# Attention and mixture of experts on one core: expert slots in another order, results fetched ahead of the next tokens

## The chip, the core and the metric

The kernel runs on one core of a Trainium2 chip. The metric is the device time of one execution in microseconds; lower is better. The core has TensorE (PE in the rows; its weight loads are PEld), VectorE (DVE), ScalarE (ACT), GpSimd (POOL) and SyncE (SP), each with its own instruction stream in order; they meet at semaphores. Transfers are issued by SP (and, for scattered rows, by GpSimd) and carried by 16 shared DMA engines.

## The reference

First an attention without softmax over 8 batches of 2496 tokens, then a layer of 8 experts, of which each token visits one.

```python
scores = scale * np.matmul(z, z.transpose(0, 2, 1))      # scale = 1 / S, S = 2496, z: (8, 2496, 64)
attn = np.maximum(scores, 0.0) ** 2
x = (u * np.matmul(attn, v)).reshape(B * S, D)            # 19968 tokens, D = 256
...
logits = x @ w_gate
e_idx = np.argmax(logits, axis=1)                         # the token's expert, of E = 8
...
for e in range(E):
    mask = e_idx == e
    h = np.maximum(x[mask] @ w1[e], 0.0)                  # 256 -> 1024
    out[mask] = gate_w[mask, None] * eom[mask, e, None] * (h @ w2[e])   # 1024 -> 256
```

## The kernel before

**Attention** takes the first 1320 us or so. Its finished tokens are sorted: GpSimd scatters each row of x, with its gate factor and its number, into `xs` in DRAM, where each expert has a region of its own.

**Slots.** The experts then run as slots. A slot is a piece of one expert's region, of a width n fixed when the kernel is built; which expert and which rows is read on the chip from small tables. There are 27 wide slots of 512 tokens from table 0 (made from the counts of the first seven batches), 3 more wide ones (table 1), seven of 480, 448, 416, 384, 352, 320 and 288 tokens (table 2), and 8 of 256 (table 3), in that order; ten further slots of 256 lie behind a condition. The last piece of an expert's tokens is covered by one of the seven, so that little is padded.

**One slot** (class `Slot`, the slot's number is `g`): `load_x` reads two values from the table and starts four transfers `sx<-xs` and one or two for `meta` (factor and number of each token). `load_w` starts eight transfers `raw<-in_w` of 256 KB, a first half `W1` and a second `W2`. There are two sets of raw buffers, so a slot's weights overwrite those of the slot two before it; if that had the same expert, a flag in the table (`cond`) skips the transfers. `split_w` cuts each weight tile into a rounded part (a ScalarE cast, L830) and the rest (a VectorE subtraction, L831). `turn` and `split_x` do the like for the tokens. `up` runs 48 matmuls in eight PSUM banks of a pool of three (`sc`, L872; two groups to a bank at 256 tokens); each bank gives `hh` (ScalarE, L881) and `hl` (VectorE, L882). `down` runs 48 more matmuls (`o`), in two halves.

**Results.** A slot of 256 has its result with tokens on partitions and scales it at once. The wider ones come out turned: VectorE transposes each half to `yt` (L945, L947), SP stores it to `yd` in DRAM (L951 to L954), and during the next slot SP reads it back in another shape, `ym` (`collect`, L967); ScalarE multiplies it by the factors (`scale`, L977, `y<-ym`) and GpSimd scatters the rows to the output.

**Order of the work.** All five engines run in the order written. `run` goes over the slots; during slot i it prepares i+1 (`split_w`, `turn`, `split_x`) and loads i+2. `up` and `down` call `then()` after each bank and twice after each half: steps 0 to 7 and 8 to 11 of a slot (six steps at 256 tokens). Each `then()` first takes one entry of the list `later`, which holds the end of attention, the making of tables 1 to 3 (`other_tables`, some twenty pieces of small VectorE instructions) and the zero rows behind each expert's last token (`pads`, nine transfers of 528 KB), and then what was put at this step with `at`. Loads of slot i+2 stand in front of step 0, its `W2` at step 3.

Of the kernel before, what the change touches and what calls it, by code (L numbers as in the profile page):

```python
# [10 lines left out]
I32 = mybir.dt.int32  # L11
AF = mybir.ActivationFunctionType
ALU = mybir.AluOpType
# [25 lines left out]
N_MAIN = 8  # L39
N_REST = MOST // E - 2 * N_FULL  # L40
LENGTHS = (N_FIRST, N_FULL, N_MID, N_REST)
WIDTHS = [TW] * (N_FIRST + N_FULL) + MID[::-1] + [T] * N_REST
NSLOT = sum(LENGTHS)
N_EXTRA = N_REST - N_MAIN

HALF = 1

# [12 lines left out]
def attention_moe(ctx, tc, zt, zq_in, ut, v, wg, w12, out):  # L60
# [437 lines left out]
    def t1(name, shape, dt=F32, tag=None):  # L498
        return pool.tile([1] + shape, dt, name=name, tag=tag or name)
# [23 lines left out]
    for i, n in enumerate(LENGTHS):  # L523
        body = n - (N_EXTRA if i == 3 else 0)
        half = -(-body // 2)
        si = t1(f"sl_i{i}", [max(n, 2 * half)], I32)
        nc.gpsimd.iota(si[:, 0 : 2 * half], pattern=[[1, half], [half, 2]], base=0, channel_multiplier=0)
        if n > 2 * half:
            nc.gpsimd.iota(si[:, 2 * half : n], pattern=[[1, n - 2 * half]], base=2 * half, channel_multiplier=0)
        elif n > body:  # L530
            nc.gpsimd.iota(si[:, body:n], pattern=[[1, n - body]], base=body, channel_multiplier=0)
        if i == 2:
            nc.gpsimd.iota(si[:, 0:n], pattern=[[-1, n]], base=n - 1, channel_multiplier=0)
        sl = t1(f"sl{i}", [n])
        nc.vector.tensor_copy(out=sl, in_=si[:, 0:n])
        places.append(sl)
# [2 lines left out]
    e8 = t1("e8", [E])  # L539
    nc.vector.tensor_copy(out=e8, in_=e8_i)  # L540

    def table(i, size, upto, step, base0, before):

        n, sl = LENGTHS[i], places[i]
        yield
        past = t1("past", [n, E])  # L550
        nc.vector.tensor_tensor(
            out=past,
            in0=sl.unsqueeze(2).to_broadcast([1, n, E]),
            in1=upto.unsqueeze(1).to_broadcast([1, n, E]),
            op=ALU.is_ge,
        )
        yield
        ex_f = t1("ex_f", [n + 2])
        if before is not None:
            nc.vector.tensor_copy(out=ex_f[:, 0:2], in_=before)  # L560
        ex_v = ex_f[:, 2:]
        nc.vector.tensor_reduce(out=ex_v.unsqueeze(2), in_=past, op=ALU.add, axis=AX.X)
        nc.vector.tensor_scalar(out=ex_v, in0=ex_v, scalar1=float(E - 1), scalar2=None, op0=ALU.min)
        yield
        nc.vector.tensor_tensor(
            out=past, in0=past, in1=step.unsqueeze(1).to_broadcast([1, n, E]), op=ALU.mult
        )
        yield
        off = t1("off", [n, 1])
        nc.vector.tensor_reduce(out=off, in_=past, op=ALU.add, axis=AX.X)  # L570
        nc.vector.tensor_scalar(out=off, in0=off, scalar1=base0, scalar2=None, op0=ALU.add)
        row = t1("row_f", [n])
        nc.vector.scalar_tensor_tensor(
            out=row, in0=sl, scalar=float(size), in1=off.rearrange("p a b -> p (a b)"), op0=ALU.mult, op1=ALU.add
        )
        yield
        return write(i, row, ex_f, before)

    def write(i, row, ex_f, before):
        name, n, ex_v = f"tab{i}", LENGTHS[i], ex_f[:, 2:]  # L580
        tab = t1(name, [3, n], I32)
        nc.vector.tensor_scalar(out=tab[:, 0], in0=row, scalar1=float(E * CAP), scalar2=None, op0=ALU.min)
        nc.vector.tensor_copy(out=tab[:, 1], in_=ex_v)
        if before is None:
            nc.vector.memset(tab[:, 2, 0:2], 1)
            nc.vector.tensor_tensor(out=tab[:, 2, 2:], in0=ex_v[:, 2:], in1=ex_v[:, : n - 2], op=ALU.not_equal)
        else:
            nc.vector.tensor_tensor(out=tab[:, 2], in0=ex_v, in1=ex_f[:, 0:n], op=ALU.not_equal)
        last = t1(name + "_last", [2])
        nc.vector.tensor_copy(out=last, in_=ex_f[:, n : n + 2])  # L590
        return tab, last

    def steps(name, row, n, size):

# [31 lines left out]
    def first_table():  # L626
        cnt = t1("cnt0", [E])
        nc.vector.tensor_tensor(out=cnt, in0=carry[0][0:1], in1=base9[:, 0:E], op=ALU.subtract)
        ns = rounded("ns0", cnt, TW, 0)
        upto = running("upto0", ns)  # L630
        st = steps("st0", base9, ns, TW)
        tabs[0], tabs["last"] = yield from table(0, TW, upto, st, 0.0, None)
        tabs["rest"] = behind("rest0", base9, capped("taken0", ns, upto, N_FIRST), TW)

    def other_tables():
# [79 lines left out]
        yield  # L715
        st = steps("st1", base1, full, TW)
        upto = running("upto1", full)
        tabs[1], tabs["last"] = yield from table(1, TW, upto, st, base1[:, 0:1], tabs["last"])
        yield
        n, sl = LENGTHS[2], places[2]  # L720
        which = t1("which", [n, E])
# [3 lines left out]
            in1=kind_of.unsqueeze(1).to_broadcast([1, n, E]),  # L725
            op=ALU.is_equal,
        )
        ex_f = t1("ex_f", [n + 2])
        nc.vector.tensor_copy(out=ex_f[:, 0:2], in_=tabs["last"])
        part = t1("part", [n, E])  # L730
        nc.vector.tensor_tensor(out=part, in0=which, in1=e8.unsqueeze(1).to_broadcast([1, n, E]), op=ALU.mult)
        nc.vector.tensor_reduce(out=ex_f[:, 2:].unsqueeze(2), in_=part, op=ALU.add, axis=AX.X)
        yield
        nc.vector.tensor_tensor(
            out=part, in0=which, in1=rest[:, 0:E].unsqueeze(1).to_broadcast([1, n, E]), op=ALU.mult
        )
        row = t1("row_f", [n])
        nc.vector.tensor_reduce(out=row.unsqueeze(2), in_=part, op=ALU.add, axis=AX.X)
        tabs[2], tabs["last"] = write(2, row, ex_f, tabs["last"])
        yield  # L740
        base3 = behind("base3", base1, full, TW)
        ns = t1("ns3", [E])
# [2 lines left out]
        upto = running("upto3", ns)  # L745
        used = tabs["used"] = t1("used", [1], I32)
        nc.vector.tensor_copy(out=used, in_=upto[:, E - 1 : E])
        tabs[3], _ = yield from table(3, T, upto, st, base3[:, 0:1], tabs["last"])

    def pads():  # L750

# [20 lines left out]
    class Slot:  # L772
        def __init__(self, g):
            self.g = g
            self.part = next(p for p in range(len(LENGTHS)) if g < sum(LENGTHS[: p + 1]))
            self.i = g - sum(LENGTHS[: self.part])
            self.n = WIDTHS[g]
            self.w = [None] * 8

        def value(self, k, top):  # L780
# [32 lines left out]
        def load_w(self, js):  # L813
            if not hasattr(self, "ex"):
                self.ex = self.value(1, E - 1)
                self.kw = {"cond": self.value(2, 1)} if 2 <= self.g <= NSLOT - N_EXTRA else {}
            wr = raw[self.g % 2]
            for j in js:
                if self.g < 2:
                    wr[j] = pool.tile([P, CH], F32, name=f"raw{j}", tag="two", bufs=16)  # L820
                nc.sync.dma_start(  # L821
                    out=wr[j],
                    in_=w12[bass.ds(self.ex, 1), :, j * CH : (j + 1) * CH].rearrange("e p f -> (e p) f"),
                    **self.kw,
                )
# [269 lines left out]
    parts = []  # L1095
    later = [idle, tail.advance] * (TAIL - 1) + [idle, lambda: parts.extend(tail.scatter())]
    later += [idle, lambda: parts.pop(0)()] * 4
    later += [idle] * (5 * 12 - len(later))
    more, fill = other_tables(), pads()
    for _ in range(27):  # L1100
        later += [idle, lambda: next(more, None), idle]
    for _ in range(E + 2):
        later += [lambda: next(fill, None)] + [idle] * 11

    def run(part, ahead=None):

        late = [j for j in W2 if part[0].w[j] is None]
        every = part + ([ahead] if ahead else [])
        for i, s in enumerate(part):
            nx = every[i + 1] if i + 1 < len(every) else None  # L1110
            nn = every[i + 2] if i + 2 < len(every) else None

            long = s.n > T
            steps = [[] for _ in range(12 if long else 6)]

            def at(k, *what):
                steps[k] += what

            for j in late:
                at(j % 4, lambda j=j: s.split_w([j]))  # L1120
            late = []
            if i and part[i - 1].n > T:
                at(2 if long else 1, part[i - 1].collect)
                at(9 if long else 4, part[i - 1].scale)
            if nn:
                nn.load_x()
                nn.load_w(W1)
                at(3, lambda: nn.load_w(W2))
            if nx:
                w = [lambda j=j: nx.split_w([j]) for j in range(8)]  # L1130
                for k, what in enumerate(
                    ([w[0]], [w[1]], [w[2]], [w[3]], [nx.turn], [w[4]], [], [], [nx.split_x], [w[5]], [w[6]], [w[7]])
                    if long
                    else ([w[0]], [w[1]], [nx.turn], [w[2]], [nx.split_x, w[3], w[4]], w[5:])
                ):
                    at(k, *what)

            def then():
                if later:
                    later.pop(0)()  # L1140
                for what in steps.pop(0):
                    what()

            s.up(then)
            s.down(then)
# [70 lines left out]
```

## Time and profile before

| what | us |
|---|---|
| median of 3 runs | 2237.5 (2236.78 to 2239.54) |
| the profiled execution, its own time | 2220.67 |
| its span | 2219.0 |
| TensorE busy | 2186.8 (99%) |
| VectorE busy | 1760.8 (79%) |
| ScalarE busy | 1441.4 (65%) |
| GpSimd busy | 935.8 (42%) |

Busy time is summed over the whole span, so 99% says nothing of single stretches. The granted clock of TensorE is 0.994 in the mean; 1 stands for 2.4 GHz, 0.5 for 1.2 GHz. The profiled execution is 16.8 us shorter than the median of the runs.

### The profile page before, as it was taken

The numbers are of one execution on the slowest core, as the hardware profiler recorded it, in microseconds if no ns is written. First come the engines' busy times: TensorE is split into PE (matmuls) and PEld (weight loads), VectorE is DVE, ScalarE is ACT, GpSimd is POOL, SyncE is SP. The second block draws the span as 40 slices with busy tenths as digits, with TensorE's granted clock in tenths as the row PEclk, the third lists the DMA queues.
The fourth block names the chain that finished last, engine by engine and source line by source line (L and its number), as shares of the span: only waits on it lengthen the run. The fifth ranks groups of instructions, "written<-read, shape, count | busy, mean of one in ns | idle before, by whom it ended". The sixth has DMA issues, their size and how long they took to land. (4 is left out here: it accounts for less than half of the span.)

```text
span 2219.0 us, 34158 instructions
## 1 busy us (share of the span) xinstructions
PE 2186.8 (99%) x10290; PEld 1851.4 (83%) x10290; DVE 1760.8 (79%) x2929; ACT 1441.4 (65%) x2271; POOL 935.8 (42%) x809
## 2 busy tenths in 40 slices
PE   9999999999999999999999999999999999999888
PEld 7888888888888888888888878888888888889888
DVE  8889889889889889889889886667566666666566
ACT  8767767767767767767767754545455555555555
POOL 0265565465566466466566565221212121111221
PEclk9999999999999999999999999999999999999999
DMA  6794794784785775876866884535554545666552
GB/s 203 190 224 157 195 218 165 202 204 167 212 190 182 208 179 193 214 163 205 211 167 202 224 162 118 154 86 143 143 144 142 146 114 166 185 193 188 160 155 63
DMA packets 435138, 384.94 MB, mean 173 GB/s; under 512 B 140637, under 2 KB 353502, under 8 KB 434944
## 3 DMA queue, kind: packets, MB, share of 16 engines
q1 hardware_dynamic: 407360, 341.09, 57.5%
q0 software_dynamic: 27584, 41.58, 6.2%
q8 instruction: 83, 1.36, 0.3%
q14 instruction: 111, 0.91, 0.1%
HBM read 281.98 MB, written 148.90 MB: 194 GB/s over the span
## 5 line engine op out<-in xcount | busy, mean ns | idle before, releaser
L467 POOL DMA_INDIRECT xs<-xr,idx x624 | 764.8, 1226 | 612.9 <-DVE idx L460 414.0
L289 PE MATMUL o<-ah,v 128*128 128x512 f32 (+1 forms) x3200 | 968.7, 386 | 0.8 <-DVE v L187 0.8
L289 PEld LDWEIGHTS o<-ah,v 128*128 128x128 f32 x3200 | 598.7, 188 | 110.0 <-DVE v L187 2.2
L289 PE MATMUL o<-al,v 128*128 128x512 f32 (+1 forms) x1520 | 586.5, 386 | 0.6 <-DVE al L226 0.3
L987 POOL DMA_INDIRECT out<-y,meta x160 | 168.1, 1051 | 660.4 <-ACT y L977 564.6
L881 ACT ACTIVATE hh<-sc 128x512 fp32r<-128x512 f32 (+7 forms) x328 | 190.4, 581 | 295.7 <-PE sc L872 294.7
L872 PE MATMUL sc<-xh,w 128*128 128x512 f32 (+8 forms) x1440 | 360.1, 366 | 17.4 <-DVE hl L882 12.0
L217 ACT ACTIVATE a<-sc 128x512 f32<-128x512 f32 (+1 forms) x480 | 251.3, 576 | 174.2 <-PE sc L216 173.2
L934 PE MATMUL o<-hh,w 128*128 128x512 f32 (+7 forms) x1184 | 357.9, 379 | 0.0
L226 DVE TENSOR_TENSOR al<-a,ah 128x1024 fp32r<-128x1024 f32 (+1 forms) x232 | 274.2, 1182 | 87.0 <-ACT ah L222 80.5
L289 PEld LDWEIGHTS o<-al,v 128*128 128x128 f32 x1520 | 285.7, 188 | 56.5 <-DVE al L226 3.2
L872 PEld LDWEIGHTS sc<-xh,w 128*128 128x128 f32 x1440 | 258.1, 191 | 60.0 <-DVE hl L882 14.8
L831 DVE TENSOR_TENSOR w<-raw,w 128x512 fp32r<-128x512 f32 x368 | 244.7, 678 | 54.4 <-ACT w L830 54.3
L934 PEld LDWEIGHTS o<-hh,w 128*128 128x128 f32 x1184 | 220.1, 188 | 38.8
L220 ACT ACTIVATE a<-a 128x1024 f32<-128x1024 f32 (+1 forms) x240 | 246.2, 1026 | 7.6
L882 DVE SCALAR_TENSOR_TENSOR hl<-sc,hh 128x512 fp32r<-128x512 f32 (+7 forms) x328 | 216.1, 661 | 43.7 <-ACT hh L881 34.8
L934 PE MATMUL o<-hl,w 128*128 128x512 f32 (+7 forms) x592 | 224.4, 379 | 0.0
L830 ACT CAST w<-raw 128x512 fp32r<-128x512 f32 x368 | 216.2, 613 | 0.0
L872 PE MATMUL sc<-xl,w 128*128 128x512 f32 (+8 forms) x720 | 204.3, 365 | 0.0
L945 DVE STREAM_TRANSPOSE yt<-o 128x512 f32<-128x512 f32 (+2 forms) x74 | 50.4, 681 | 176.4 <-PE o L934 160.5
L215 PE MATMUL sc<-z,hl 128*128 128x512 f32 (+1 forms) x480 | 184.0, 383 | 2.6 <-ACT a L217 1.8
L216 PE MATMUL sc<-z,hl 128*128 128x512 f32 (+1 forms) x480 | 183.1, 381 | 0.0
(185 smaller groups left out, 2419.0 us busy)
## 6 DMA issues: line engine op xcount, KB each, us to landing
raw<-in_w SPq DMA_DIRECT2D x368, 256.0 KB
td<-t SPq DMA_DIRECT2D x160, 512.0 KB
z<-td SPq DMA_DIRECT2D x640, 128.0 KB
raw<-in_v SPq DMA_DIRECT2D x72, 256.0 KB
u<-in_ut SPq DMA_DIRECT2D x32, 512.0 KB
ym<-yd SPq DMA_DIRECT2D x126, 128.0 KB
sx<-xs SPq DMA_DIRECT2D x120, 128.0 KB
yd<-yt SPq DMA_DIRECT2D x30, 512.0 KB
```

Source lines behind the costliest of these rows:

```text
L215: nc.tensor.matmul(out=sc[:, :w], lhsT=st, rhs=ll[:, :w], start=True, stop=False)
L217: nc.scalar.activation(out=a[:, q, :w], in_=sc[:, :w], func=AF.Relu)
L220: nc.scalar.activation(out=a[:, :, :w], in_=a[:, :, :w], func=AF.Square)
L226: nc.vector.tensor_tensor(out=al[:, :, :w], in0=a[:, :, :w], in1=ah[:, :, :w].bitcast(F32), op=ALU.subtract)
L289: nc.tensor.matmul(out=o[d][:, :w], lhsT=vv[:, q, dd], rhs=rhs, start=begins and q == 0 and k == 0, stop=ends and q == 1 and k == len(term ...
L467: it = nc.gpsimd.indirect_dma_start(out=xs[:, :], out_offset=bass.IndirectOffsetOnAxis(ap=idx[:, n : n + 1], axis=0), in_=self.xr[:, n, :] ...
L830: nc.scalar.copy(out=ww[:, 0], in_=wr)
L831: nc.vector.tensor_tensor(out=ww[:, 1], in0=wr, in1=ww[:, 0].bitcast(F32), op=ALU.subtract)
L872: nc.tensor.matmul(out=hp[:, at : at + n], lhsT=wb[2 * d + f // 4][:, ww, fs], rhs=xx[:, d, :], start=k == 0, stop=k == 5,)
L881: nc.scalar.activation(out=ho, in_=hp[:, 0:used], func=AF.Relu)
L882: nc.vector.scalar_tensor_tensor(out=lo, in0=hp[:, 0:used], scalar=0.0, in1=ho.bitcast(F32), op0=ALU.max, op1=ALU.subtract)
L934: nc.tensor.matmul(out=yp[:, :n], lhsT=wb[4 + f // 2][:, ww, ds_], rhs=hx[:, :n], start=k == 0, stop=k == 23,)
```

## The change

- **Order of the slots.** `sequence()` writes it out: sixteen wide slots; then four times a wide slot and a narrow one (288, 320, 352 and 384 tokens, slots 17, 19, 21 and 23); the remaining ten wide ones; 480, 448 and 416 tokens; the eight of 256. The widths are the same set as before.
- **Order of the loads in a slot.** Before: tokens of slot i+2, its `W1`, at step 2 (1 at 256 tokens) `collect` of slot i-1, at step 3 `W2`. Now: `W1`, `collect`, the tokens, at step 3 `W2`.
- **`scale`** moves from step 9 to step 10 (at 256 tokens it stays at step 4).
- **Weights** are fetched under the flag only for slots 2 to 15 and the third to ninth slot of 256; all others fetch always. So the tables no longer pass on the last two experts of the one before.
- **`later`**: the tables begin after 48 steps and not 60, and take every second step and not every third; the pads come every sixth step and not every twelfth.

```diff
@@ constants
-WIDTHS = [TW] * (N_FIRST + N_FULL) + MID[::-1] + [T] * N_REST
...
+N_RUN = 16
+def sequence():
+    wide = [(0, i) for i in range(N_FIRST)] + [(1, i) for i in range(N_FULL)]
+    got, wide = wide[:N_RUN], wide[N_RUN:]
+    for i in range(4):
+        got += [wide.pop(0), (2, i)]
+    return got + wide + [(2, i) for i in reversed(range(4, N_MID))] + [(3, i) for i in range(N_REST)]
...
@@ class Slot
-            self.n = WIDTHS[g]
+            self.part, self.i = ORDER[g]
+            self.n = (TW, TW, MID[min(self.i, N_MID - 1)], T)[self.part]
...
-                self.kw = {"cond": self.value(2, 1)} if 2 <= self.g <= NSLOT - N_EXTRA else {}
+                again = 2 <= self.g < N_RUN or (self.part == 3 and 2 <= self.i <= N_MAIN)
+                self.kw = {"cond": self.value(2, 1)} if again else {}
...
@@ the list later
-    later += [idle] * (5 * 12 - len(later))
+    later += [idle] * (4 * 12 - len(later))
...
-    for _ in range(27):
-        later += [idle, lambda: next(more, None), idle]
+    for _ in range(29):
+        later += [idle, lambda: next(more, None)]
     for _ in range(E + 2):
-        later += [lambda: next(fill, None)] + [idle] * 11
+        later += [lambda: next(fill, None)] + [idle] * 5
@@ run
             if i and part[i - 1].n > T:
-                at(2 if long else 1, part[i - 1].collect)
-                at(9 if long else 4, part[i - 1].scale)
+                at(10 if long else 4, part[i - 1].scale)
+            if nn:
+                nn.load_w(W1)
+            if i and part[i - 1].n > T:
+                part[i - 1].collect()
             if nn:
                 nn.load_x()
-                nn.load_w(W1)
                 at(3, lambda: nn.load_w(W2))
```

**Queue SP, the start of a slot.** Before, in the slot of 384 tokens (`yd` and `ym` belong to the slot ahead, `sx`, `meta` and `raw` to the one two behind; TENSOR_LOAD reads a value from a table):

```order
L951 DMA yd<-yt 128x768
L952 DMA yd<-yt 128x192
L781 TENSOR_LOAD tab_17858
...
L796 DMA sx<-xs 32x12x64
...
L804 DMA meta<-xs 128x3x2
L781 TENSOR_LOAD tab_17858
...
L821 DMA raw_14917<-in_w 128x512
...
L967 DMA ym<-yd 32x4x256 x3
L967 DMA ym<-yd 32x4x192
L821 ISA
L821 DMA raw_15048<-in_w 128x512
```

Now, in the slot of 288 tokens:

```order
L958 DMA yd<-yt 128x1024
L784 TENSOR_LOAD tab_17319
...
L825 DMA raw_14915<-in_w 128x512
...
L971 DMA ym<-yd 32x4x256 x4
L784 TENSOR_LOAD tab_17319
...
L799 DMA sx<-xs 32x10x64
...
L807 DMA meta<-xs 128x2x2
L810 DMA meta<-xs 64x2
L825 ISA
L825 DMA raw_15046<-in_w 128x512
```

The four transfers `ym` have moved from behind tokens, values and first weights to behind one value and the first weights, and the tokens stand behind them.

**ScalarE, the middle of a slot** (`hh` of the slot itself, `xh` and `w` of the next, `y` of the one ahead). Before, the slot of 384 tokens:

```order
L881 ACTIVATE hh<-sc 128x384 x2
L847 CAST xh<-xf 128x2x352
L977 ACTIVATE y<-ym,meta 128x256 x3
L977 ACTIVATE y<-ym,meta 32x256
L830 CAST w<-raw_14763 128x512
L830 CAST w<-raw_14804 128x512
L830 CAST w<-raw_14885 128x512
L881 ACTIVATE hh<-sc 128x352
```

Now, the slot of 288 tokens between wide ones:

```order
L885 ACTIVATE hh<-sc 128x288 x2
L851 CAST xh<-xf 128x1024
L834 CAST w<-raw_14761 128x512
L981 ACTIVATE y<-ym,meta 128x256 x4
L834 CAST w<-raw_14802 128x512
L834 CAST w<-raw_14883 128x512
L885 ACTIVATE hh<-sc 128x512
```

One weight cast has moved from behind `y<-ym` to ahead of it.

**VectorE, the making of the tables.** Two of its pieces, `has` to the last `pairs` and `quads` to `base`, before:

```order
L882 SCALAR_TENSOR_TENSOR hl<-sc,hh 128x512 x2
L700 TENSOR_SCALAR has<-kind_of 1x8
...
L709 TENSOR_SCALAR pairs<-pairs 1x8
L848 TENSOR_TENSOR xl<-xf,xh 128x1024
L945 STREAM_TRANSPOSE yt<-o 128x4x4x32
L831 TENSOR_TENSOR w<-raw_15088,w 128x512
L507 TENSOR_SCALAR quads_c<-pairs 1x8
...
L621 SCALAR_TENSOR_TENSOR base_17364<-width_of,rest_14343 1x8
L831 TENSOR_TENSOR w<-raw_15142,w 128x512
L945 STREAM_TRANSPOSE yt<-o 128x4x4x32
```

The same two pieces now:

```order
L886 SCALAR_TENSOR_TENSOR hl<-sc,hh 128x512
L705 TENSOR_SCALAR has<-kind_of 1x8
...
L714 TENSOR_SCALAR pairs<-pairs 1x8
L835 TENSOR_TENSOR w<-raw_14628,w 128x512
L886 SCALAR_TENSOR_TENSOR hl<-sc,hh 128x512
L835 TENSOR_TENSOR w<-raw_14649,w 128x512
L886 SCALAR_TENSOR_TENSOR hl<-sc,hh 128x512
L520 TENSOR_SCALAR quads_c<-pairs 1x8
...
L626 SCALAR_TENSOR_TENSOR base_17005<-width_of,rest_14341 1x8
L835 TENSOR_TENSOR w<-raw_14683,w 128x512
L886 SCALAR_TENSOR_TENSOR hl<-sc,hh 128x512
```

Before, the two pieces stood on both sides of `xl` and a transpose `yt`, in the second half of a slot; now both stand in the first half, with two `hl` between them.

## Rows read from the trace of the kernel before

**Rows 1.** Busy time per engine (instructions) in stretches; granted clock, DMA share, GB/s.

```profile
core 0: us, PE busy (x) PEld busy (x) DVE busy (x) ACT busy (x) POOL busy (x), PEclk, DMA share, GB/s
1890.00:1975.00 85.00, 85.00 (x377) 70.38 (x376) 54.56 (x78) 45.93 (x84) 15.11 (x16) 1.00 0.71 194
2033.66:2105.33 71.67, 63.92 (x385) 61.86 (x385) 43.58 (x86) 37.31 (x81) 15.45 (x14) 0.95 0.55 157
2105.33:2140.54 35.21, 27.22 (x196) 26.59 (x195) 17.91 (x30) 17.64 (x35) 9.73 (x9) 0.85 0.58 160
2140.54:2209.66 69.12, 69.11 (x576) 68.91 (x575) 51.45 (x85) 46.59 (x90) 11.66 (x12) 1.00 0.35 100
2047.00:2051.00 4.00, 4.00 (x25) 4.00 (x24) 0.58 (x1) 0.00 (x0) 0.00 (x0) 1.00 0.89 299
```

**Rows 2.** TensorE's waits from 1960 us on: total us, times, longest.

```profile
PE sc L872 <- DVE hl L882: 10.4, 5, 3.9
PE sc L872 <- ACT xh L847: 5.4, 1, 5.4
```

**Rows 3.** ScalarE's timeline: start, us, line, instruction, [idle before <- releaser].

```profile
1926.46 1.71 ACT L977 ACTIVATE y<-ym,meta 128x256 f32<-128x256 f32 x4 [3.80 <-DMA ym<-yd]
...
2053.78 1.71 ACT L977 ACTIVATE y<-ym,meta 128x256 f32<-128x256 f32 x4 [8.83 <-DMA ym<-yd]
...
2124.86 1.30 ACT L977 ACTIVATE y<-ym,meta 128x256 f32<-128x256 f32 x3 [5.88 <-DMA ym<-yd]
```

**Rows 4.** TensorE's timeline: first matmuls of two slots, and two that waited.

```profile
1953.56 0.62 PE L872 MATMUL sc<-xh,w 128*128 128x512 f32 x2
...
1975.32 0.59 PE L872 MATMUL sc<-xh,w 128*128 128x480 f32 x2
...
2058.88 0.61 PE L872 MATMUL sc<-xh,w 128*128 128x352 f32 x2 [3.91 <-DVE hl L882]
...
2126.72 0.79 PE L872 MATMUL sc<-xh,w 128*128 128x256 f32 x2 [5.38 <-ACT xh L847]
```

**Rows 5.** Queue SP's timeline (issues), the first slot of 256 tokens.

```profile
2111.20 0.33 SPq L951 DMA_DIRECT2D yd<-yt  x1
2111.57 0.47 SPq L952 DMA_DIRECT2D yd<-yt  x1
...
2117.03 2.26 SPq L821 DMA_DIRECT2D raw<-in_w  x4
```

**Rows 6.** Queue SP's timeline, the wide slot from 1910 us.

```profile
1910.99 0.33 SPq L954 DMA_DIRECT2D yd<-yt  x1
1912.19 2.00 SPq L796 DMA_DIRECT2D sx<-xs  x4
...
1916.50 2.25 SPq L821 DMA_DIRECT2D raw<-in_w  x4
1918.79 1.85 SPq L967 DMA_DIRECT2D ym<-yd  x4
```

**Rows 7.** Queue SP's timeline, the slot of 384 tokens.

```profile
2038.91 1.91 SPq L796 DMA_DIRECT2D sx<-xs  x4
...
2045.67 2.27 SPq L821 DMA_DIRECT2D raw<-in_w  x4
```

**Rows 8.** VectorE's timeline: table instructions, and the instruction behind each set.

```profile
1465.86 0.14 DVE L700 TENSOR_SCALAR has<-kind_of 1x8 f32<-1x8 f32 x1
...
1466.89 1.23 DVE L848 TENSOR_TENSOR xl<-xf,xh 128x1024 fp32r<-128x1024 f32 x1
...
1470.81 0.15 DVE L507 TENSOR_SCALAR quads_c<-pairs 1x8 int32<-1x8 f32 x1
...
1472.36 0.69 DVE L831 TENSOR_TENSOR w<-raw,w 128x512 fp32r<-128x512 f32 x1
```

**Rows 9.** Queue SP's timeline: first weights of slots 16 and 26, skipped.

```profile
1633.64 1.21 SPq L821 DMA_DIRECT2D raw<-in_w  x4
...
1851.21 1.57 SPq L821 DMA_DIRECT2D raw<-in_w  x4
```

More of the change, by code (lines that the diff above doesn't have):

```diff
@@ L41 @@
 LENGTHS = (N_FIRST, N_FULL, N_MID, N_REST)
-WIDTHS = [TW] * (N_FIRST + N_FULL) + MID[::-1] + [T] * N_REST
-NSLOT = sum(LENGTHS)
 N_EXTRA = N_REST - N_MAIN
+N_RUN = 16
[5 more added lines that the diff above has]
+    return got + wide + [(2, i) for i in reversed(range(4, N_MID))] + [(3, i) for i in range(N_REST)]
+ORDER = sequence()
+NSLOT = len(ORDER)
 HALF = 1
@@ L532, in attention_moe @@
         if i == 2:
-            nc.gpsimd.iota(si[:, 0:n], pattern=[[-1, n]], base=n - 1, channel_multiplier=0)
+            nc.gpsimd.iota(si[:, 0:n], pattern=[[1, n]], base=0, channel_multiplier=0)
         sl = t1(f"sl{i}", [n])
@@ L540, in attention_moe, with table @@
     nc.vector.tensor_copy(out=e8, in_=e8_i)
-    def table(i, size, upto, step, base0, before):
+    def table(i, size, upto, step, base0):
         n, sl = LENGTHS[i], places[i]
@@ L557, in table @@
         yield
[L558 to L561, printed above, removed]
+        ex_v = t1("ex_v", [n])
         nc.vector.tensor_reduce(out=ex_v.unsqueeze(2), in_=past, op=ALU.add, axis=AX.X)
@@ L576, in table, with write @@
         yield
[L577 to L581, printed above, removed]
+        return write(i, row, ex_v)
+    def write(i, row, ex_v):
+        n = LENGTHS[i]
+        tab = t1(f"tab{i}", [3, n], I32)
         nc.vector.tensor_scalar(out=tab[:, 0], in0=row, scalar1=float(E * CAP), scalar2=None, op0=ALU.min)
         nc.vector.tensor_copy(out=tab[:, 1], in_=ex_v)
[L584 to L591, printed above, removed]
+        nc.vector.memset(tab[:, 2, 0:2], 1)
+        nc.vector.tensor_tensor(out=tab[:, 2, 2:], in0=ex_v[:, 2:], in1=ex_v[:, : n - 2], op=ALU.not_equal)
+        return tab
     def steps(name, row, n, size):
@@ L631, in first_table @@
         st = steps("st0", base9, ns, TW)
-        tabs[0], tabs["last"] = yield from table(0, TW, upto, st, 0.0, None)
+        tabs[0] = yield from table(0, TW, upto, st, 0.0)
         tabs["rest"] = behind("rest0", base9, capped("taken0", ns, upto, N_FIRST), TW)
@@ L717, in other_tables @@
         upto = running("upto1", full)
-        tabs[1], tabs["last"] = yield from table(1, TW, upto, st, base1[:, 0:1], tabs["last"])
+        tabs[1] = yield from table(1, TW, upto, st, base1[:, 0:1])
         yield
@@ L727, in other_tables @@
         )
-        ex_f = t1("ex_f", [n + 2])
-        nc.vector.tensor_copy(out=ex_f[:, 0:2], in_=tabs["last"])
+        ex_v = t1("ex_v", [n])
         part = t1("part", [n, E])
         nc.vector.tensor_tensor(out=part, in0=which, in1=e8.unsqueeze(1).to_broadcast([1, n, E]), op=ALU.mult)
-        nc.vector.tensor_reduce(out=ex_f[:, 2:].unsqueeze(2), in_=part, op=ALU.add, axis=AX.X)
+        nc.vector.tensor_reduce(out=ex_v.unsqueeze(2), in_=part, op=ALU.add, axis=AX.X)
         yield
@@ L738, in other_tables @@
         nc.vector.tensor_reduce(out=row.unsqueeze(2), in_=part, op=ALU.add, axis=AX.X)
-        tabs[2], tabs["last"] = write(2, row, ex_f, tabs["last"])
+        tabs[2] = write(2, row, ex_v)
         yield
@@ L747, in other_tables @@
         nc.vector.tensor_copy(out=used, in_=upto[:, E - 1 : E])
-        tabs[3], _ = yield from table(3, T, upto, st, base3[:, 0:1], tabs["last"])
+        tabs[3] = yield from table(3, T, upto, st, base3[:, 0:1])
     def pads():
@@ L774, in __init__ @@
             self.g = g
-            self.part = next(p for p in range(len(LENGTHS)) if g < sum(LENGTHS[: p + 1]))
-            self.i = g - sum(LENGTHS[: self.part])
-            self.n = WIDTHS[g]
+            self.part, self.i = ORDER[g]
+            self.n = (TW, TW, MID[min(self.i, N_MID - 1)], T)[self.part]
             self.w = [None] * 8
```

## The prediction

> **What bounds the kernel now.** Read the windows first. TensorE's row is full nearly everywhere; the question is only where it is not. In the wide slots it is busy all of 85 us, and in the last six narrow slots 69.11 of 69.12 us, but in the two windows between them, from the slot of 384 tokens to the second slot of 256, it is busy 63.92 of 71.67 and 27.22 of 35.21 us [rows 1]. So all that a new order of slots can give back lies in these 107 us; the rest only has to stay as it is. The waits say who was late: VectorE five times for `hl`, ScalarE once for `xh` [rows 2]. Neither is slow. The chain is seen at one stall, the longest but one.
>
> The result of a slot goes out to `yd` and comes back as `ym`, and `scale` (`y<-ym`) stands on ScalarE in the middle of the next slot. ScalarE works in order, so all behind `scale` waits with it: three casts of the next weights, then `hh` of the next slot; VectorE waits for those casts, and `hl` is behind them. In the slot of 384 tokens `scale` stood for 8.83 us until 2053.78 [rows 3], and TensorE, which has three score banks to run ahead with, went on at 2058.88, that is 5.1 us later, after 3.91 us idle [rows 4]. Each late `scale` also makes VectorE's second transpose late, so the next `yd` is late too: the first narrow 256 slot begins at 2105.33 (the window's edge), and its `yd` is issued only at 2111.20 [rows 1, 5].
>
> Why is `ym` late? In the undisturbed wide slot that begins at 1910.04 (1953.56 less two slots of 1975.32 - 1953.56 = 21.76 us) the queue SP shows it [rows 3, 4, 6]: `yd` issued at 1910.99 and done issuing at 1911.32, then the next-but-one slot's tokens `sx` from 1912.19, weights from 1916.50, and only then `ym` at 1918.79; `scale` starts at 1926.46, 16.4 us after the slot's start. A slot of 512 has time for that. The limit, for a slot that takes t and is followed by one whose three banks take b, is t + b - 5.1 us after its start. With b = 18/96 of 21.76 = 4.1 us and t in proportion to the width: 20.8 us for 512 before 512, but about 11 us for 288 tokens.
>
> **The loss to be had.** First window: 71.67 - 63.92 = 7.75 us idle, and a granted clock of 0.95 (part of the time 1.2 in place of 2.4 GHz), some 5% of 71.67 = 3.6 us more. Second: two slots of 256 take 2 x 69.12/6 = 23.04 us where nothing waits, and took 35.21: 12.2 us, of which 2.61 and 5.38 us are waits (10.4 of `hl` in all, less 7.75, and the one for `xh`), and 4.2 us goes with a granted clock of 0.85 (stretches at 1.2 in place of 2.4 GHz after the waits), so about 2.1 us per long wait [rows 1, 2]. Together **23.5 us**.
>
> **The change part by part.**
>
> *Results before tokens (`collect` before `load_x`).* Weights may now start where `sx` started: in the wide slot 1912.19 in place of 1916.50, 4.3 us earlier; in the 384 slot 2038.91 in place of 2045.67, 6.8 us [rows 6, 7]. `ym` follows the weights as before. So `scale` can start 16.4 - 4.3 = 12.1 us after a slot's start. Bound below: the 0.5 MB of `sx` no longer moves ahead of it either, at 299 GB/s [rows 1] 1.7 us, so 10.4 us. Bound above: the store `yd` must have landed before `ym` may be issued; so far 7.5 us lay between them (1911.32 to 1918.79), now about 3.1 (a register load of 0.87 and 2.25 us of weights). No row shows a landing of `yd`; the nearest, `ym` itself, took from 1920.64 (its last issue) to 1926.46, 5.8 us. With 5.8 the issue is held until 1910.99 + 5.8 = 1916.8, and `scale` starts 1916.8 + 1.85 + 5.8 = 1924.5, 14.4 us after the start. I take 12: half a megabyte at 299 GB/s is 1.8 us, nearer to 3.1 than to 5.8. Behind a held `ym` on SP wait `sx` of two slots on and the second half of its weights, needed a whole slot later: no one waits for them.
> The Trainium skill, "DMA: Bandwidth & Descriptors", "Two DMAs through the same engine are not ordered" speaks against the edit: the issuing engine has to wait for the first transfer's semaphore before it issues one that depends on it, so SP now stands with everything behind it. The same page ("Anatomy of one DMA") gives a fixed 2.0 us and 436 GB/s per transfer, by an estimate 3.2 us for this store; by that the hold is nothing, and the sum below stays. No row here shows the wait.
>
> *`scale` one step later.* One cast with its subtraction fewer stands behind it, on VectorE 0.69 us [rows 8], some of it under the casts; I take 0.5, so 5.1 becomes 4.6 and the limits rise: 288 tokens 12.2 + 4.1 - 4.6 = 11.7 us, 320 tokens 13.1, 352 tokens 14.5.
>
> *The order.* 288, 320, 352 and 384 now stand with a wide slot on each side, so that a lag isn't passed on: the wide slot's limit is 21.3. At 12 us only 288 is short, by **0.3 us** (0 to 2.7). 480, 448 and 416 have limits of 17 and more.
>
> *416 before the first 256.* This neighbourhood stays, and so does its stall, smaller. There `xh`, which TensorE needs at once, stands behind `scale`: 2126.72 - 2124.86 = 1.86 us [rows 3, 4]. `scale` was at 2124.86; `yd` will be issued about 1 us after the slot's start as in the wide slot and not 5.87 (4.9 less), and the weights start about 1.6 us after `yd` (two register loads) and not 2117.03 - 2112.04 = 5.0 (3.4 less) [rows 5]. So `scale` at 2116.6, 11.2 us after 2105.33, TensorE 13.1, the slot's own time 11.52: **1.6 us** (0 to 3.9), and for the clock 1.0 (0 to 2.1).
>
> *Tables earlier and denser.* Their small VectorE instructions came every third step from slot 5; now every second from slot 4. Then two groups fall in one slot between `hl` of banks 1 and 4: six take 1466.89 - 1465.86 = 1.03 us, nine 1472.36 - 1470.81 = 1.55 us [rows 8]. In such a slot a bank takes 21.76/16 = 1.36 us; `hl` and one weight subtraction leave only about 0.15 us of that free, so 2.6 us of inserts stand against some 2 us that TensorE is ahead by its three banks (an estimate, 3 x 1.36 less the chain of `hh` and `hl`): **0.7 us** (0 to 2.6). The removed copies are single instructions of 0.15 us; nothing.
>
> *Weights always fetched from slot 16.* Eight of the slots 16 to 26 now skip their weights (issues of 1.2 to 1.6 us in place of 2.25; first and last in [rows 9]). 8 x 2.1 = 16.8 MB more. In the window where every slot loads, DMA runs at 194 GB/s with a share of 0.71 and TensorE waits for nothing [rows 1]: nothing, if that cover holds. A pair of 288 and 512 has 34.0 us for 4.2 MB of weights and 800 tokens x 4 KB = 3.3 MB: 220 GB/s, a share of about 0.8. The pads, two to a slot and not one, are 0.5 MB each in slots 8 to 13, ahead of this; nothing.
>
> **Sum.** 23.5 - 0.3 - 1.6 - 1.0 - 0.7 = 19.9, so the profiled 2220.67 us becomes 2200.8. The runs' median is 2237.5, 16.8 above the profiled one; I take the gain as the same there: **2217.6**.
>
> **Rivals.**
> *The store holds the fetch* (14.4 us above). 288 waits 2.7, 320 1.3, the second 256 slot 14.4 + 1.86 - 11.52 = 4.7; with three clock losses of 2.1 and the tables, 15.7. Gain 8: 2229.5. For it: 5.8 us is the only landing near it. Against: that transfer had 1 MB of weights and `sx` around it.
> *The fetch comes no earlier:* its time is set by the traffic. At 16.4 us 288 waits 4.7, 320 3.3, 352 1.9, 384 0.5, the 256 slot 6.7, with four clock losses 25.5 against 23.5: no change, 2239. Against: of the 16.4 us in the wide slot, 5.8 lie behind the last issue of `ym` and 5.2 (1911.32 to 1916.50) in what no longer stands ahead of it [rows 3, 6].
> *Slower:* the added weights. If the engines could hold no more than the 194 GB/s they show, a pair would take 7.5 MB / 194 = 38.7 us and not 34.0: 4 x 4.7 = 19, with a clock loss for each 27, against 20: 2245. It decides at 220 GB/s. Against: 299 over four us, at a share of 0.89 [rows 1].
>
> **Chances.** Forecast (14 to 25 us gained) 0.69; store 0.18 (5 to 14); no earlier 0.07; slower 0.06. The forecast alone reaches from 2212.5 (all 23.5 and what the clock row rounds off) to 2223.5; with most of the store's case 2212 to 2229.5. A change under 0.2% (4.5 us) can't be told from none here. Faster 0.88, same 0.06, slower 0.06.
>
> **What would show it.** Right: SP issues weights, `ym`, `sx` in this order, `scale` 10.5 to 12.5 us after a slot's start; no wait over 0.5 us at the four interleaved slots; one of 1 to 2 us before the second 256 slot; waits of under 1 us in slots 4 and 5. Wrong: `ym` issued long after the weights (store), `scale` idle as before (no earlier), TensorE or VectorE waiting for `raw` in slots 16 to 27 (slower).

## The result, and the profile after

The changed kernel takes 2211.45 us (median of 4 runs, 2208.46 to 2214.83), the kernel before, beside it, 2237.14 (4 runs, 2235.78 to 2239.54): ratio 0.9884 [0.9866, 0.9903], 25.7 us less. The forecast was 2217.6, with 2212.0 as the low end of the range. The profiled execution took 2209.45 us, 11.2 less than that of before.

TensorE's windows of the changed kernel, with the columns of [rows 1]: wide slots, the stretch with the four interleaved narrow slots, from the slot of 416 to the third of 256, and the last six of 256.

```profile
1890.00:1975.00 85.00, 85.00 (x377) 70.38 (x376) 55.37 (x80) 45.68 (x84) 15.72 (x16) 1.00 0.78 199
1677.49:1846.14 168.65, 168.65 (x866) 148.98 (x865) 113.05 (x186) 94.83 (x185) 32.16 (x32) 1.00 0.81 209
2082.23:2128.57 46.34, 43.61 (x290) 42.68 (x288) 28.54 (x50) 25.62 (x51) 11.05 (x11) 0.96 0.61 174
2128.57:2197.85 69.28, 69.28 (x578) 69.07 (x576) 51.62 (x85) 46.57 (x90) 11.66 (x12) 1.00 0.37 103
```

The second row is the result: 168.65 us with the slots of 288, 320, 352 and 384 in them, and TensorE busy in all of it, at full clock, with DMA at 209 GB/s. Where the two windows of [rows 1] had 7.75 and 8.0 us of idle time, only the third row here keeps some: 2.7 us, of which 2.1 are one wait for `xh`. TensorE's waits from 1200 us on (total, times, longest):

```profile
PE sc L876 <- DVE hl L886: 2.7, 5, 0.9
PE sc L876 <- ACT xh L851: 2.1, 1, 2.1
PE o L302 <- ACT ah L283: 1.5, 1, 1.5
PE o L938 <- issue: 1.4, 5, 0.3
```

Before, `hl` was 10.4 us from 1960 on alone, and `xh` 5.4 [rows 2]. The 2.7 us of `hl` are another 2.7 than the idle time of the third row: all five lie in the first six slots, two of them in the slots with tables (0.16 and 0.65 us). One of 0.33 us lies in the slot ahead of those, where VectorE has no table instruction but stands ("issue" is time in which the engine waited for nothing that the profile shows):

```profile
1401.62 0.69 DVE L886 SCALAR_TENSOR_TENSOR hl<-sc,hh 128x512 fp32r<-128x512 f32 x1 [1.71 <-issue]
```

ScalarE, whose wait for `ym` stood ahead of all this, shows the cause gone. From 1600 us on, in the kernel before it waited for `ym`

```profile
ACT y L977 <- DMA ym<-yd: 80.8, 19, 8.8
```

and in the changed kernel

```profile
ACT y L981 <- DMA ym<-yd: 9.1, 6, 2.6
```

SP's timeline in the changed kernel shows why, first in the slot of 288 (it starts at 1699.25), then in the first of 256 (2100.32):

```profile
1700.19 0.33 SPq L958 DMA_DIRECT2D yd<-yt  x1
1701.39 2.07 SPq L825 DMA_DIRECT2D raw<-in_w  x4
1703.56 1.79 SPq L971 DMA_DIRECT2D ym<-yd  x4
1706.51 1.97 SPq L799 DMA_DIRECT2D sx<-xs  x4
...
2101.22 0.33 SPq L955 DMA_DIRECT2D yd<-yt  x1
2101.60 0.43 SPq L956 DMA_DIRECT2D yd<-yt  x1
2103.97 2.40 SPq L825 DMA_DIRECT2D raw<-in_w  x4
2106.47 1.79 SPq L971 DMA_DIRECT2D ym<-yd  x4
```

`ym` is issued 3.04 us after the store's issue ended (1700.52 to 1703.56; before 7.5 us in [rows 6]) and SP does not wait in between. `scale` in the same two slots (ScalarE's timeline):

```profile
1710.79 1.71 ACT L981 ACTIVATE y<-ym,meta 128x256 f32<-128x256 f32 x4 [2.63 <-DMA ym<-yd]
...
2111.82 1.70 ACT L981 ACTIVATE y<-ym,meta 128x256 f32<-128x256 f32 x4 [2.21 <-DMA ym<-yd]
```

That is 11.5 us after the start of both slots; the prediction had 12 and 11.2. Compare the longest idle time ahead of `scale` before, 8.83 us [rows 3].

### The profile page after: what moved, and what is told of

It reads as the page before. It is cut to its first block, busy times and chain, and to the rows that moved or that the text cites. A ratio compares the mean times of both kernels' runs of the same rounds, so it can differ in the third digit from the quotient of the medians.

```text
span 2207.1 us, 34237 instructions
## 1 busy us (share of the span) xinstructions
PE 2183.3 (99%) x10290; PEld 1845.2 (84%) x10290; DVE 1759.0 (80%) x2925; ACT 1439.4 (65%) x2271; POOL 928.4 (42%) x809
## 4 chain that ended last, share of the span: by engine, by line
PE 91%; DVE 4%; DMA 2%; issue 1%; ACT 1%; SPq 0%; DVEq 0%; ACTq 0%
PE o L302 43%; PE sc L876 18%; PE o L938 17%; PE sc L228 4%; PE sc L229 4%; PE o L910 2%; PE mp L353 2%; DMA raw<-in_w 1%; DMA z<-td 1%; DVE al L239 0%; DVE w L835 0%; DVE hl L886 0%; DVE t L251 0%; DMA ym<-yd 0%; DMA sx<-xs 0%
## 5 line engine op out<-in xcount | busy, mean ns | idle before, releaser
L991 POOL DMA_INDIRECT out<-y,meta x160 | 160.4, 1002 | 647.1 <-ACT y L981 549.3
```

## The experiments

The kernel before ran beside every experiment, at 2222.6 to 2224.0 us in four of the later comparisons and 2243.6 in one. Ratios and differences below are always to its runs in the same comparison.

**Each half of the change alone** (e1 to e4, one chip; before 2223.05 there). e1 is the kernel before, unchanged. e2 is the kernel before with the new order of loads and `scale` at step 10, and nothing else:

```diff
-                at(2 if long else 1, part[i - 1].collect)
-                at(9 if long else 4, part[i - 1].scale)
+                at(10 if long else 4, part[i - 1].scale)
             if nn:
-                nn.load_x()
                 nn.load_w(W1)
+            if i and part[i - 1].n > T:
+                part[i - 1].collect()
+            if nn:
+                nn.load_x()
                 at(3, lambda: nn.load_w(W2))
```

e3 is the changed kernel with the same lines turned back. e4 is the kernel before with all weights fetched:

```diff
-                self.kw = {"cond": self.value(2, 1)} if 2 <= self.g <= NSLOT - N_EXTRA else {}
+                self.kw = {}
```

> The kernel before, unchanged: its time against itself, and a second trace of it. The profiled execution shown of it took 2220.67 us, its timed runs 2235.8 to 2239.5; the changed kernel's runs and its trace agree (2208 to 2215, 2209.45). Theory: the 16 us between trace and runs lie before the slots, in attention or in the first two slots, which the change does not touch, so this trace shows the slots from the third on taking 844 us again and any difference ahead of them. Rival: they lie in the narrow slots, whose waits grow from run to run; then this trace, if it takes about 2237 us, shows 860 us there. Ratio 1.000 within 0.1% for both.

> The kernel before with the new order of loads in a slot alone (first weights, results, tokens; scaling one step later), and the old order of the slots. Theory: the order of the loads is what counts. With the scaling about 12 us after a slot's start, the limits of neighbouring narrow slots are 16.6 (416 tokens), 15.0, 13.4, 11.9 and 12.3 us (288), so they hardly wait, and only the second slot of 256 waits, some 2 us: 16 to 20 us faster than before, about the whole gain in the trace. Rival: narrow slots side by side pass their lag on, and the gain needs the wide slots between them: under 8 us faster.

> The changed kernel with the old place of the results' fetch and of the scaling (behind tokens and first weights, scaling a step earlier); slots, weights and tables as changed. Theory: the fetch still ends some 16.4 us after a slot's start, so 288, 320, 352 and 384 tokens wait 4.7, 3.3, 1.9 and 0.5 us and the second slot of 256 6 us or more, with the clock lost after them: no gain, within 5 us of the kernel before, to either side. Rival: a wide slot behind each narrow one takes the lag up: 8 us faster or more.

> The kernel before with every slot fetching its weights, whether it has them or not, and nothing else changed: some 40 slots, of which about 28 skip them now, fetch 2.1 MB more each. Theory: the queues carry it under TensorE's work: 0, at most 3 us slower. Rival: it delays the results' fetch of the wide slots until they wait too: 10 us slower or more.

| run | median us | ratio | from the third slot to the last matmul, in the trace |
|---|---|---|---|
| e1 | 2222.8 | 1.0002 [0.9993, 1.0012] | 845.7 |
| e2 | 2202.25 | 0.9909 [0.9895, 0.9923] | 824.8 |
| e3 | 2219.82 | 0.9985 [0.9976, 0.9993] | 844.9 |
| e4 | 2223.6 | 1.0004 [0.9995, 1.0013] | 844.5 |

The load order with `scale` one step later gives 20.8 us (the two were not run apart). Slot order, weights and tables without it give 3.2 in the runs, and 0.7 in the traces of e1 and e3. The added weights cost nothing that can be measured. TensorE's waits from 1600 us on, first of e2, with `scale` early and the old slot order:

```profile
PE sc L872 <- ACT xh L847: 2.8, 1, 2.8
PE sc L872 <- DVE xl L848: 0.2, 1, 0.2
```

then of e3, with `scale` late and the new slot order:

```profile
PE sc L876 <- ACT xh L851: 9.0, 1, 9.0
PE sc L876 <- DVE hl L886: 8.3, 4, 4.0
```

In e3 the waits behind 288, 320 and 352 are 3.98, 2.95 and 0.74 us, none behind 384; the rival "the fetch comes no earlier" had 4.7, 3.3, 1.9 and 0.5 by its limits. So the limits were right to 1.2 us (they are made for `scale` one step later; at e3's step each is 0.5 us lower). The slots behind narrow ones wait in either order as long as `scale` is late; in e2, where it is early, none does before the second slot of 256.

**The changed kernel again, and the wait that is left** (e5 to e8, one chip; before 2224.0). e5 is the changed kernel, e6 the kernel before, both unchanged. e7 is e2, and e8 the changed kernel, each with `scale` one step later in the slots of 256, so that it stands behind the casts of the next tokens (`xh`):

```diff
-                at(10 if long else 4, part[i - 1].scale)
+                at(10 if long else 5, part[i - 1].scale)
```

> The changed kernel, unchanged. Its first runs were 25.7 us below the kernel before where that took 2237 us; its trace is only 11.2 us below the trace of before. Theory: the machine, not the change, makes the kernel before take 2223 or 2237 us, and the change is worth what the slots show, 17 to 20 us, where it takes about 2223; the trace has 844 - 827 = 17 us less from the third slot on, with 2.2 us given back in the slots that make the tables. Rival: the change is worth 25 us wherever it runs, and the trace of before was a lucky one.

> The kernel before once more, for a trace beside that of the changed kernel in the same place. If its runs take about 2237 us: theory, attention and the first two slots are some 5 us longer than in the first trace and the waits of the narrow slots longer too; rival, all 16 us lie in attention. If they take about 2223 us it repeats the second trace, slots from the third on 845 us, within 2 us.

> The kernel before with the order of loads changed, in the old order of the slots, and scaling behind the token split in the slots of 256 (its last step there). Theory: the one wait left, 2.80 us before the second slot of 256, goes, and with it the lost clock: the first two slots of 256 take 23 to 24 us in place of 27.9, 24 to 26 us faster than before. Rival: the three weight casts now behind the scaling become late and TensorE waits in the second half of the second slot instead: 20 to 22 us faster, as without it.

> The changed kernel with the scaling behind the token split in the slots of 256. Theory: as above, the wait of 2.11 us before the second slot of 256 goes: 4 to 5 us faster than the changed kernel, so 21 to 24 us faster than before where that takes 2223 us. Rival: no more than 1 us faster than the changed kernel.

e5: 2202.78 us, 0.9904 [0.9888, 0.9921], so 21.2 less; from the third slot to the last matmul 825.8 against 845.7 in e1 and e6 (e6: 2223.25, 0.9998): 19.9. e7: 2199.04, 0.9887 [0.987, 0.9903]; e8: 2199.56, 0.989 [0.9873, 0.9906]. The wait for `xh` is gone in both; in e7 (TensorE's timeline) another has come in its place:

```profile
2112.22 0.51 PE L872 MATMUL sc<-xh,w 128*128 128x256 f32 x2 [2.20 <-DVE hl L882]
```

The first two slots of 256 take 27.7 us in e5, 25.5 in e7 and 24.2 in e8, against 23.0 where nothing waits. So `scale` ahead of `xh` did cost what the prediction said it would in kind, and 3 us can be had back (4 to 5 were expected; in e8 a wait of 0.90 us for `hl` is left). e7 and e8 have the lowest medians of the study; the two can't be told apart, and neither can e2 and e5. So at a time of 2223 or 2224 us for the kernel before, no gain of the new slot order can be seen once the fetch is early.

**How much room the fetch has** (e9, e10), **and two arrangements** (e11, e12; one chip; before 2243.55 there). e9 is the kernel before and e10 the changed kernel, each with 512 KB more copied from DRAM to an unused place in DRAM, on SP just ahead of each `collect`:

```diff
+            junk = dram.tile([P, 1024], F32, name="junk", bufs=4)
+            nc.sync.dma_start(out=junk, in_=w12[0:1, :, 0:1024].rearrange("e p f -> (e p) f"))
             of = self.yd.rearrange("(a r) m q y -> m r a (q y)", r=32)
```

e11 is the changed kernel with the tables at every third step again; e12 is e2 with `scale` in the slots of 256 behind the last casts of the next weights:

```diff
-    for _ in range(29):
-        later += [idle, lambda: next(more, None)]
+    for _ in range(22):
+        later += [idle, lambda: next(more, None), idle]
```

```diff
-                at(10 if long else 4, part[i - 1].scale)
+                if long:
+                    at(10, part[i - 1].scale)
...
+            if i and part[i - 1].n > T and not long:
+                at(5, part[i - 1].scale)
```

> The kernel before with one more transfer of 512 KB, from the weights to an unused place in DRAM, on SP just ahead of each slot's fetch of results: the fetch ends some 2 us later in every slot, as it might on a machine with slower transfers. Theory: the kernel before has no room, and each of its seven narrow slots and the second of 256 pass the 2 us on: 10 to 18 us slower than the kernel before. That would let the 25.7 us of the first comparison, where the kernel before took 2237 us, be the same change under slower transfers. Rival: the lags overlap and only the last one counts: 2 to 5 us slower.

> The changed kernel with the same added transfer ahead of each fetch of results. Scaling stood 10.7 to 11.1 us after the start of the interleaved narrow slots, against limits of 11.7 (288 tokens) and 13.1 (320), and 12.3 us after that of the first slot of 256, where every microsecond counts. Theory: 288 waits 1 us, the second slot of 256 2 us more: 3 to 5 us slower than the changed kernel, 16 to 18 us faster than before as it stands. Rival: it loses as much as the kernel before with that transfer, 10 us or more.

> The changed kernel with the tables made at every third step again, from the same first step. Theory: the pieces no longer meet between the banks of one slot; of the 0.33, 0.15 and 0.65 us of waits in the two slots that make them only the 0.15 stays, 1.1 us faster than the changed kernel, that is 22 us faster than before where that takes 2223 us. Rival: nothing, the waits come from the total of the pieces.

> The kernel before with the new order of loads, and in the slots of 256 the scaling behind the last weight casts as well as behind the token split. Theory: the 2.20 us wait for hl that came in the second slot of 256 when the scaling stood ahead of those casts goes too, and both slots take 23.1 us: 27 us faster than before where that takes 2223 us. Rival: hh of the second slot waits behind the scaling and the 2 us stay: 24 to 25 us faster.

e9: 2261.27, 1.0095 [1.0075, 1.0114], 17.7 us more than the kernel before, within the 10 to 18 of its theory. TensorE's waits from 1600 us on grew from 18.6 us in e1 to

```profile
PE sc L872 <- DVE hl L882: 26.2, 7, 6.2
PE sc L872 <- ACT y L979: 7.0, 1, 7.0
```

e10: 2229.34, 0.9933 [0.9919, 0.9948]. Its waits there:

```profile
PE sc L876 <- ACT xh L851: 5.7, 1, 5.7
PE sc L876 <- issue: 1.1, 1, 1.1
PE o L910 <- DVE hl L886: 0.4, 2, 0.2
```

Against traces from other chips, e9 has 14.6 us of new waits (33.2 - 18.6, e1) and e10 4.3 (7.2 - 2.9, e5). Of the 4.3, 2.8 lie before the second slot of 256, and 1.1 is a wait for "issue" of the kind that the last experiments take up. From the sixth slot to the last matmul, clock included, e9 takes 802.3 against 780.4 us and e10 765.7 against 759.8. The changed kernel itself did not run beside them; its nearest relation, e11, took 2220.69, 8.7 us less than e10, where the theory had 3 to 5 against the changed kernel. So the interleaved slots have some 2 us of room that the slots of before had not. E2 with the extra transfer was not tried, so whether the new slot order is a part of that room stays open.

e11: 2220.69, 0.9905 [0.989, 0.9919]. Of the two waits in table slots only one of 0.15 us is left, and the two slots take 1.2 us less than in e5 (22.21 and 21.76 against 22.44 and 22.70), as the theory had it. But waits of 1.8 and 3.6 us stand in other early slots, which the last experiments take up, so its time says nothing on the tables. e12: 2222.76, 0.9899 [0.9883, 0.9915]. No wait for `xh`, but the two slots took 28.1 us and not 23.1, with 2.3 us for `hh`. ScalarE's row shows what held that `hh`:

```profile
2136.66 0.60 ACT L881 ACTIVATE hh<-sc 128x512 fp32r<-128x512 f32 x1 [4.26 <-remote]
```

This is no wait for `scale` or a cast, but one of the kind that the last experiments take up, so e12 does not decide between its theory and its rival. It shows something else: with the old slot order the slots of 352 and 288 took 16.37 and 14.10 us there (15.46 and 13.19 in e2); in e11, beside it and in the new order, 15.46 and 13.18. The new order may thus be worth a little where a kernel runs longer; with one trace of each this is not shown.

**Why 25.7 here and 21.2 there** (e13 to e16: twice both kernels, unchanged, one chip).

> The kernel before, unchanged, for a trace beside that of e14 on one chip. Theory: the gain is the fetch moved ahead in the narrow slots, and it is larger where the kernel before takes longer, since a slower transfer lengthens the waits behind the narrow slots; on a chip where this kernel takes 2236 or more, the stretch from slot 2 to the last matrix multiplication would be above 847 us (845.5 in e1 and e6), with more waiting ahead of the narrow slots than 18.7 us. Rival: the extra time lies in the attention and the first five slots alone, the same for both kernels, and the stretch from slot 5 on is as in e1; then the difference between 25.7 and 21.2 is the spread of runs. On a chip where it takes 2223 it would be as e1 and tell nothing of this.

> The changed kernel, unchanged, on the same chip as e13. Theory: 25 us or more below the kernel before where that takes 2236 or more, 21 us where it takes 2223; slots from the second on 825.6 us on either. Rival: 21 us below on any chip, the rest being spread between runs.

> As e13, on whichever chip is given: that one took 2222.6 and so told nothing of the chips on which the kernel before takes 2236 or more. Theory: on such a chip the narrow slots (from the fifth slot on) wait more than in e1, and the extra gain is there. Rival: from the fifth slot on the trace is as in e1, and the extra time lies ahead of it.

> As e14. Theory: 25 us or more below the kernel before where that takes 2236 or more. Rival: 19 to 21 us below, as in e5 and e14, wherever it runs.

e13: 2222.68, 1.0004; e14: 2203.83 against 2222.55, 0.9912 [0.9896, 0.9929], 18.7 us less. e15: 2222.18, 0.9999; e16: 2203.0 against 2223.79, 0.9911 [0.9897, 0.9925], 20.8 less. The kernel before never took 2236 us or more here, so the theory of a larger gain there stays untested on the two unchanged kernels. From the third slot to the last matmul the traces give 844.9 against 825.8 us, and 844.1 against 826.3.

What the traces do show is where the changed kernel and its relations lose time when they run longer. In the changed kernel's own first profile, ScalarE waited between 1321 and 1437 us, in the first five slots:

```profile
ACT hh L885 <- issue: 8.8, 6, 7.5
ACT hh L885 <- remote: 5.8, 2, 3.6
```

and in e11, from 1316 to 1450 us:

```profile
ACT hh L885 <- issue: 15.5, 4, 7.6
ACT hh L885 <- remote: 7.8, 3, 3.0
```

Sums of 14.6 to 25.9 us of this kind stand in that stretch in the first profile of the changed kernel and in e9 to e12, and none in the profile shown ahead of the prediction, in e1 to e8 and in e13 to e16. In the changed kernel's first profile the matmuls from the third slot on start 5 us later than in e16 (1370.60 against 1365.55); in e9, the kernel before with the extra transfer, the first five slots take 122.5 us, in e1 112.2. Behind the fifth slot little is left of it: from the sixth to the last matmul the changed kernel's first profile takes 760.7 us and e11 759.9, against 759.8 in e5. So in the changed kernel this time lies ahead of the slots in which it gains. For the kernel before, e9 alone has it, and there the extra transfer is mixed in.

## Why the prediction was right and wrong

**The mechanism was right, and the sum too, on the time it was made from.** By the new order of the loads `scale` was to come 12 us after a slot's start ("I take 12"): it came after 11.5 in two slots of the changed kernel, 10.65 and 11.1 in the slots of 288 and 320 of e5. Its price, 19.9 us, is 19.9 between the traces of e1 and e5, 19.1 and 17.8 between the later pairs, and 18.7, 20.8 and 21.2 us in runs. From a median of 2223 the same sum gives 2203, and there the changed kernel takes 2202.8 to 2203.8. That the total is hit so closely is in part luck: the loss to be had was 2.2 us larger than taken, and what is left of it 2.15 us larger (the terms below).

**The step that failed** is the last one: "The runs' median is 2237.5, 16.8 above the profiled one; I take the gain as the same there". The profile was of an execution of 2220.67 us, and its rows explain nothing of the 16.8. The low end of the range had no term for that: it was the loss to be had and what the clock row rounds off, and the time came out 0.55 us below it. The rows were sound for the places where the kernel before takes 2223 us; the step from there to 2237 had none behind it.

What the runs showed in its place: at 2222.6 to 2224.0 us the gain is 18.7 to 21.2 us; in the one comparison at 2237.14 it is 25.7, 5.8 more than the sum. A longer time need not make it larger: at 2243.55 the relations e11 and e12 gained 22.9 and 20.8 us. One ratio of 0.990 lies in all four intervals of the two unchanged kernels, so the rest may be the spread of runs. Or the kernel before lost more than the changed one in the first comparison. Of the changed kernel it is known where: against e5 its first profile has 2.0 us more ahead of the first slot, 3.1 in the first five slots and 0.9 behind them. The kernel before took some 14 us more there than at 2223, and no trace of it unchanged at such a time was to be had, so where these lie, in the first slots or in the narrow ones, and with it the cause of the extra 5.8 us, stays open.

**Terms of the sum:**
- Loss to be had, 23.5: what was gained and what is left are 16.9 + 5.2 + 1.8 = 23.9 in the two traces first compared, and 19.9 + 4.6 + 1.15 = 25.7 between e1 and e5 (the second 256 slot and the tables are the terms below; 0.6 of the 1.8 is the early slot with the wait of 0.33 us and has no term). With 25.7 the range's low end would have held the time.
- The slot of 288, 0.3: no wait in any trace of the changed kernel.
- The second slot of 256, 1.6 + 1.0 = 2.6: 28.25 - 23.04 = 5.2 us in the changed kernel's first trace, with a wait of 2.11, and 27.66 - 23.04 = 4.6 in e5, with one of 2.85. `scale` came 11.5 and 12.3 us after the slot's start and not 11.2. In both the weights start 1.9 us behind the end of the last store's issue (2102.03 to 2103.97 in the rows of SP) and not 1.6; in e5 `scale` also came 4.3 us after the last issue of `ym`, in the first trace 3.6. The loss by the clock was taken too low as well (last section).
- The tables, 0.7: in e5 two slots took 22.44 and 22.70 us for 21.76, in e1 one took 22.23: 0.68 + 0.94 - 0.47 = 1.15.
- Added weights, 0: e4. The cover named for them, DMA at a share of 0.8, is 0.81 in the second window.

**The rivals.** The store does not hold the fetch. A rule was weighed here: the Trainium skill, "DMA: Bandwidth & Descriptors", "Two DMAs through the same engine are not ordered", has SP wait for the store. The rule is no obstacle where the store lands in time: SP's list of waits for e5 has one for `yd` ahead of `ym`, of 0.5 us, and the changed kernel's first has none. The estimate of 3.2 us for a landing, worked out in the prediction from the same page's "Anatomy of one DMA", rests on a fit that the page gives for transfers issued by GpSimd, while SP issued this store. It is not contradicted: `ym` was issued 3.37 us after the start of the store's issue (1700.19 to 1703.56) without a wait. "The fetch comes no earlier" fell with the rows of `scale`. E3, where it does come late, comes out 3.2 us faster than before, near the "no change" that this rival had. "Slower through added weights" fell in e4.

## What to carry to other kernels

Where engines work in order, look for the transfer on which an instruction waits in the middle of other work, and ask what was issued ahead of it that nobody needs yet: fetching the results ahead of the tokens, with `scale` one step later, gave all of the gain that can be measured here. Before a gain is carried from a profile to a median, ask what the profile has not got: where both differ by more than the runs spread, the difference has a cause of its own, and the range has to hold it.

## What the runs showed of the hardware

The same kernel took 2222.6 to 2224.0 us in four comparisons, on three chips, 2237.1 in one and 2243.6 in another, each within 5 us of its median (one run of e13 lies 7.3 us above). Of the longer ones there is no trace of that kernel itself. But the five traces taken beside them (the changed kernel's first, e9 to e12) have waits on ScalarE and VectorE put down to "issue" and "remote" that the others hardly have (11 us at `y<-o` apart, which all have). They stand all along the execution: on ScalarE 15.0 to 48.1 us of them ahead of 1316 us, during attention, where the other traces have 0.2 at most. In e11, up to 1316 us and from 1450 us on:

```profile
ACT a L230 <- issue: 16.7, 12, 3.3
DVE yt L949 <- issue: 43.9, 18, 3.5
```

It is mainly in the first five slots, where they reach 7.6 us at once, that TensorE comes late by them: these slots take 116.0 to 128.7 us in the five traces and 112.1 to 112.9 in the others. What the engines wait for there the profile doesn't say.

A wait of 2.85 us on TensorE cost more than itself. Windows of e5, the first two slots of 256, with the columns of [rows 1]:

```profile
2094.95:2109.47 14.52, 11.67 (x97) 11.47 (x97) 6.45 (x12) 6.66 (x14) 1.18 (x2) 0.99 0.66 178
2109.47:2122.61 13.14, 13.14 (x96) 12.92 (x97) 10.60 (x17) 8.85 (x17) 5.79 (x6) 0.88 0.56 169
```

The first slot ends with the 2.85 us in which TensorE stands; in the second it is busy all the time and yet takes 13.14 us where such a slot takes 11.52, at a granted clock of 0.88: a part of it ran at 1.2 in place of 2.4 GHz. That is 1.6 us on top, where the prediction had 1.0.
